# Attention and expert kernel on one core: a planner's cost, a new order of the work, and a shorter count at the end

## The chip, the cores and the metric

The kernel runs on one core of one Trainium2 chip. The metric is the device time of one execution in microseconds (us). The core has five instruction queues that run side by side: TensorE (PE in the profile; its weight loads have a row of their own, PEld), VectorE (DVE), ScalarE (ACT), GpSimd (POOL) and SyncE (SP), which here issues nearly all transfers (DMAs). An engine works through its queue in order; a semaphore holds an instruction until what it needs is there.

## The reference, cut to what matters

```python
# q: 4 x 12288 x 128, kv: 4 x 384 x 32 x 128 (H x W x C)
k = v = kv.reshape(B, H//4, 4, W//4, 4, C).mean(axis=(2, 4)).reshape(B, -1, C) @ w_sr     # 768 keys
a = softmax(q @ k.T / sqrt(C));  x = a @ v                        # 49152 tokens x 128
logits = x @ w_gate                                               # 8 experts
e = argmax(logits);  gate = softmax(logits)[e]
out = gate * (relu(x @ w1[e]) @ w2[e])                            # 1024 hidden units
```

## The kernel before, in words

The tokens are cut into 96 blocks of 512, 24 for each of the four batches `b`; a block is called `t` here. For a block the kernel

- loads q (`qr`, line 987), splits it on POOL into a high and a low f16 part (`qp`, lines 1001 and 1003), and has a transfer on SP turn it (`qT`, line 1005, a DMA transpose: "a turning"; line 1081 is the same for x);
- forms scores on PE in three steps of two matmuls (`s.t.0` to `s.t.2`, L387 into tile `s`), the exponent on ACT (`e`, line 1020), and on DVE `r` (line 1022), which leaves out what a second-moment matrix `M` gives;
- sums the values on PE in four parts (`po`), splits them (`xp`, on ACT and DVE or, by a switch, on POOL) and turns them (`x`);
- runs the batch's usual expert on PE: hidden units `ph.t.0` to `ph.t.2` into one of two PSUM banks (tile `b`), `relu` on ACT and POOL (`gf`, `gh`, `g`), and the way back `py.t`, also in a bank `b`;
- multiplies by the gate on DVE (`ys`, line 1148, tile `y`) and stores on SP (`out_dram<-y`, line 1151).

Beside the blocks runs the work for the next batch: its kv is loaded in three groups of four 512 KB transfers (line 453), pooled, and made into keys (`KT`), and its expert's units are sorted and gathered. For batch 0 this stands at the start: pairs of loaded tiles are added on DVE (`two`, line 463), PE sums and turns them (`pt`, into tile `s`, 16 records each), and the keys follow by way of ACT (`pT`), PE (`pk`, matmul `b<-pT,wsr`), ACT (`vT`) and DVE. Matmuls on `slots` are fillers that keep PE going while it has nothing else.

Tokens whose expert is another one are counted and done by `general_step`, three times within the program (for batches 0 to 2), and in a loop at the end as often as a count `n_left` says. The count: `lp` holds numbers per partition, PE sums them over partitions (`pc`, line 1269), DVE copies them (`left`) and makes numbers of steps (`steps`, `ends`, `n_left`, lines 1489 to 1495); then every engine reads `n_left`, and the program ends.

The order of the instructions of all engines is made before the launch by a planner (`Plan`). Every piece of work is an `op` with an engine, an estimated duration, a due time, what it needs and gives, and its buffers. `Plan.order` (line 170 on) is a list scheduler: on each engine it takes, among the ops that can start, the one with the earliest due time, and gives out buffers in that order. The table `NUDGE` shifts due times by kind of op, by block, or for one op; the table `WAYS` says for some ops which engine does them (`u` of a block: its third group of hidden units is checked and left out of `py`; `x`: the split of x on POOL; `l`: the logits' copy on DVE; `a`, `b`, `c`, `d`: single conversions per batch). For a turning the planner adds to its time on SP half of the time by which the transfers already issued reach beyond the next 2.5 us:

```python
end = free[o.eng] = start + o.us + (0.5 * max(0.0, moved - start - 2.5) if o.eng == "SP" and 1.2 < o.us < 1.8 else 0.0)
```

Here `moved` is the time at which the planner thinks that all transfers issued so far have moved. Nothing of the planner runs on the chip: only its order does.

Of the kernel before, what the change touches and what calls it, by code (L numbers as in the profile page):

```python
# [73 lines left out]
mw:-29.5 nofl:-2.5 o:140 ok.48:-85.5 own2:-13 own?.48:-25 pT.2:14.5 pU:9 pX:0.5 pd:-48 perm.5:12 perm.6:-46 pf.72:-110
pl:-39.5 po.1:1.5 po.2:0.5 pooled.1:3.5 px:-14 qTh:7 qh:3 qp:3 qr:180.5 r.0:-39.5 r.1:0.5 rest:21.5 rs:-7.5 se:-9
see:-68 some0:30.5 sum.0.2.1:2 sum.1.1.1:-6 sum.1.2.0:-2 sum.1.3.0:3.5 sum.2.2.0:-1 sum.2.2.1:4.5 sum.2.3.0:1.5
sure.0:4.5 uy:10.5 uy0:15 w:-29.5 w1l:33.5 w2U:-9.5 w2h:4.5 ws0:-70.5 x:15 xh:1.5 xl:-23.5 ys:0.5 =D.0:-15.5
=D.13:-0.5 =D.5:8 =Lh.3:33.5 =Ms.0:-124.5 =drs.13:-24 =e.10.0:-20 =e.37.1:-2 =e.53.2:9 =e.84.0:20.5 =fl.28:15.5
# [5 lines left out]
=lg.58:-13.5 =lg.8:3 =lgc.3:10 =lp.1.24:53 =mk.1.24:2 =mk2.3.72:16 =mom.3:10.5 =own.3:6.5 =own2.1:7 =pW.2:7 =pX.0:12.5
=pY.3:4 =perm.0.3:-13.5 =perm.0.4:-36.5 =perm.0.5:-14 =perm.0.7:-32.5 =perm.3.5:-2.5 =ph.11.1:8 =ph.15.0:-6
=ph.20.2:-3.5 =ph.21.2:17.5 =ph.24.0:-1 =ph.25.0:-2 =ph.26.1:6.5 =ph.30.0:-29 =ph.35.2:3.5 =ph.37.0:2 =ph.38.2:-3
=ph.39.0:-1.5 =ph.45.1:11 =ph.46.0:12.5 =ph.46.2:-3 =ph.47.2:1 =ph.48.0:10 =ph.49.1:-9.5 =ph.50.1:6.5 =ph.51.0:4.5
=ph.57.0:-7.5 =ph.58.0:-5.5 =ph.59.1:2.5 =ph.6.2:1.5 =ph.61.0:3 =ph.61.1:0.5 =ph.61.2:-2 =ph.64.1:-5.5 =ph.65.0:-6.5
# [1473 lines left out]
```

## Time and profile before

| | us |
|---|---|
| median of 3 runs | 786.45 (785.96 to 789.99) |
| profiled execution | 786.58 |
| its span | 784.5 |
| PE busy in the span | 739.5 (94%) |
| DVE, ACT, POOL busy | 639.1, 588.0, 577.3 |

The span runs from the first instruction to the last; 2.08 us of the profiled execution lie around it. The granted PE clock is at its upper level (2.4 GHz) throughout, except in the last 3.5 us, in which PE has no work. A wait in brackets in a timeline is the idle time of the engine before the instruction, and who ended it.

### The profile page before, as it was taken

What the parts mean: (1) busy time and instruction counts of PE and PEld (TensorE: products, weight loads), DVE (VectorE), ACT (ScalarE), POOL (GpSimd) and SP (SyncE); (2) the same over time, 40 slices, a digit from 0 to 9 for tenths busy, and PEclk for the clock granted to TensorE, in tenths of its full rate; (3) what the DMA queues carried; (4) which work ended last, traced back from release to release, by engine and by line L of the source; (5) the groups of instructions that cost most, each with busy time, mean ns of one, the idle gap of its engine ahead of it and who ended that gap; (6) DMA issues with size and microseconds to landing.
All of it is one profiled execution on the core that took longest, in us unless ns stands there. A gap on an engine that the chain in (4) does not pass through costs nothing.

```text
span 784.5 us, 21744 instructions
## 1 busy us (share of the span) xinstructions
PE 739.5 (94%) x8399; PEld 580.3 (74%) x8399; DVE 639.1 (81%) x1262; ACT 588.0 (75%) x968; POOL 577.3 (74%) x803
## 2 busy tenths in 40 slices
PE   5997999999999899999999899999999999999995
PEld 5675776887777677778776776878877777787774
DVE  5789876889988888868968888688898898767685
ACT  1367778879778777777787787778878787878783
POOL 0357879878789888886779978888656957686662
PEclk9999999999999999999999999999999999999999
DMA  9676989995798999797569899799575889668441
GB/s 341 166 204 115 223 191 204 198 199 114 156 231 175 228 205 264 154 210 134 122 139 225 205 240 248 158 192 192 136 166 106 171 176 200 151 122 166 93 105 56
DMA packets 326168, 138.90 MB, mean 177 GB/s; under 512 B 212478, under 2 KB 318082, under 8 KB 326064
## 3 DMA queue, kind: packets, MB, share of 16 engines
q1 hardware_dynamic: 325584, 137.27, 78.0%
q8 instruction: 66, 1.08, 0.6%
q14 instruction: 38, 0.31, 0.1%
q0 software_dynamic: 192, 0.17, 0.1%
q10 hardware_dynamic: 288, 0.07, 0.0%
HBM read 59.12 MB, written 26.94 MB: 110 GB/s over the span
## 4 chain that ended last, share of the span: by engine, by line
PE 64%; DVE 9%; ACT 8%; DMA 8%; POOL 5%; issue 3%; SPq 0%; ACTq 0%; POOLq 0%; DVEq 0%
PE b L387 31%; PE po L387 19%; PE s L387 13%; DMA qT<-qp 4%; DVE r L1022 4%; ACT e L1020 3%; POOL kv L478 1%; DMA x<-xp 1%; DMA kv<-in_kv_dram 1%; DMA gp<-in_q_dram,gi 1%; ACT X L1113 1%; ACT g L1121 1%; DVE y L1148 1%; DVE xp L1057 1%; ACT junk L742 1%
## 5 line engine op out<-in xcount | busy, mean ns | idle before, releaser
L1022 DVE SCALAR_TENSOR_TENSOR r<-s,e 128x1024 bf16<-128x1024 f32 x288 | 346.8, 1217 | 63.7 <-ACT e L1020 61.6
L1020 ACT ACTIVATE e<-s 128x1024 f32<-128x1024 f32 x288 | 292.1, 1029 | 62.6 <-PE s L387 59.0
L387 PE MATMUL po<-v,r 128*128 128x145 f16 x2304 | 251.4, 227 | 2.6 <-DVE xp L1057 1.7
L387 PEld LDWEIGHTS <-r 128*128 128x128 bf16 x2304 | 167.0, 98 | 26.7 <-issue 4.9
L387 PE MATMUL s<-qT,KT 128*128 128x512 f16 x576 | 166.8, 379 | 11.6 <-DVE r L1022 7.7
L387 PE MATMUL b<-w2U,g 128*128 128x128 f16 x1664 | 156.5, 219 | 1.0 <-POOL g L1117 0.6
L387 PE MATMUL b<-x,w1U 128*128 128x512 f16 x465 | 139.4, 379 | 9.0 <-ACT g L1121 4.7
L387 PE MATMUL po<-M,qT 128*128 128x136 f16 x1152 | 130.9, 223 | 0.0
L387 PE MATMUL b<-L,x 128*128 128x128 f16 x1116 | 123.0, 219 | 1.1 <-ACT g L1121 0.7
L1003 POOL TENSOR_TENSOR qp<-qr,qp 128x512 f16<-128x512 f32 x94 | 108.9, 1159 | 15.6 <-DVE gi L1314 2.0
L1117 POOL TENSOR_TENSOR g<-X,g 128x512 f16<-128x512 f32 x94 | 108.8, 1158 | 10.8 <-DVE gg L1451 4.1
L387 PEld LDWEIGHTS <-g 128*128 128x128 f16 x1664 | 109.0, 98 | 1.9 <-POOL g L1117 1.4
L387 PEld LDWEIGHTS <-qT 128*128 128x128 f16 x1152 | 84.5, 98 | 27.6 <-issue 5.1
L1121 ACT ACTIVATE g<-b,zb 128x512 f16<-128x512 f32 x128 | 87.5, 692 | 18.3 <-PE b L387 15.3
L1001 POOL CAST qp<-qr 128x512 f16<-128x512 f32 x94 | 58.7, 625 | 47.7 <-DMA qr<-in_q_dram 25.3
L387 PEld LDWEIGHTS <-x 128*128 128x128 f16 x1116 | 80.9, 98 | 16.8 <-issue 5.4
L387 PEld LDWEIGHTS <-KT 128*128 128x128 bf16 x576 | 51.3, 99 | 48.0 <-issue 14.1
L1113 ACT ACTIVATE X<-b,zb 128x512 f32<-128x512 f32 x94 | 65.2, 696 | 19.5 <-PE b L387 19.5
L478 POOL TENSOR_TENSOR kv<-kv,kv 128x512 f32<-128x512 f32 x54 | 68.0, 1272 | 15.4 <-DMA kv<-in_kv_dram 6.1
L1115 POOL CAST g<-X 128x512 f16<-128x512 f32 x94 | 58.2, 620 | 28.3 <-ACT X L1113 13.1
L387 PEld LDWEIGHTS <-w1U 128*128 128x128 f16 x480 | 45.2, 98 | 40.5 <-issue 9.2
L1148 DVE TENSOR_TENSOR y<-b,gt 128x512 f32<-128x512 f32 x96 | 65.2, 680 | 7.8 <-PE b L387 5.8
(376 smaller groups left out, 961.2 us busy)
## 6 DMA issues: line engine op xcount, KB each, us to landing
qr<-in_q_dram SPq DMA_DIRECT2D x96, 256.0 KB, 3.4
out_dram<-y SPq DMA_DIRECT2D x96, 256.0 KB, 2.7
kv<-in_kv_dram SPq DMA_DIRECT2D x41, 512.0 KB, 6.1
raw<-in_moe_w_dram SPq DMA_DIRECT2D x14, 512.0 KB, 5.1
e<-in_kv_dram SPq DMA_DIRECT2D x3, 512.0 KB, 9.1
v_dram<-vT SPq DMA_DIRECT2D x4, 384.0 KB, 3.1
qT<-qp SPq DMA_TRANSPOSE x94, 3.6
x<-xp SPq DMA_TRANSPOSE x91, 3.5
```

The lines of the kernel that those rows point to most:

```text
L387: return nc.tensor.matmul(o, l, r, start=start, stop=stop)
L478: nc.gpsimd.tensor_add(flat(to), flat(to), flat(of))
L742: op("ACT", 1.25, lambda j=j, junk=junk: nc.scalar.activation(junk.tile, krow.tile, AF.Sign, bias=key(j), scale=-1.0, accum_out=lc(j)), at ...
L1001: op("POOL", .62, lambda: nc.gpsimd.tensor_copy(qp.tile[:, 0], qr.tile), T - 1.9 * LEN, [("qr", t)], [("qh", t)], [qr, qp])
L1003: op("POOL", 1.17, lambda: nc.gpsimd.tensor_sub(qp.tile[:, 1], qr.tile, qp.tile[:, 0]), T - 1.8 * LEN, [("qh", t)], [("qp", t)], [qr, qp])
L1020: op("ACT", 1.03, lambda e=e, ps=ps: nc.scalar.activation(e.tile, ps.tile, AF.Exp), at + .6, [("s", t, s)], [("e", t, s)], [ps, e])
L1022: op("DVE", 1.22, lambda e=e, ps=ps, s=s: nc.vector.scalar_tensor_tensor(r.tile[:, 2 * s:2 * s + 2], ps.tile, 1.0, e.tile, op0=ALU.add, op ...
L1113: op("ACT", .69, lambda ph=ph, zu=zu: nc.scalar.activation(gf.tile, ph.tile, AF.Relu, bias=zu()), at + .5, [("ph", t, u), ("zb", b)], [("g ...
L1115: op("POOL", .62, lambda: nc.gpsimd.tensor_copy(gg.tile[:, 0], gf.tile), at + 1.5, [("gf", t)], [("gh", t), ("g", t)], [gf, gg])
L1117: op("POOL", 1.16, lambda: nc.gpsimd.tensor_sub(gg.tile[:, UH], gf.tile, gg.tile[:, 0]), at + 2, [("gf", t), ("gh", t)], [("g", t)], [gf, gg])
L1121: op("ACT", .69, lambda u=u, ph=ph, zu=zu: nc.scalar.activation(gg.tile[:, u], ph.tile, AF.Relu, bias=zu()), at + .5, [("ph", t, u), ("zb" ...
L1148: op("DVE", .69, lambda: nc.vector.tensor_tensor(y.tile, py.tile.rearrange("p (c d) -> p c d", d=C), bc(gr["gt"].tile[:, 0, js], C), op=AL ...
```

## The change

The cost of a turning behind transfers that are backed up is counted in full (factor 1 for 0.5), the last op `rest` gets a landing time, and `NUDGE` and `WAYS` hold other numbers, so that all five queues stand in another order. `WAYS` has 63 blocks with `u` for 64, 39 with `x` for 35, 46 with `l` for 50; `a3` and `c3` are gone, `d0` stands for `d3`. The counts, which are whole numbers below 257, are read by PE as the upper halves of their f32 words, in bf16, in `pc` and in two products of `general_step` (`pb`, `pr`); the copy `left` and the number of steps take one instruction less each; the last block (t = 95) is multiplied and stored in two halves, the second of them issued by ACT.

```diff
-L:46.5 M:-43.5 cbc:25 cg:237.5 e.0:3.5 e.1:3 e.2:-1.5 ex:47.5 g:0.5 gate:31 general.0.done:17 general.0.h4:10
+KT:-91 L:37 Ls:6.5 Mh:22.5 con:8.5 drs:-37 e.0:3 e.1:4.5 e.2:-2.5 ex:79.5 fl:2.5 g:0.5 gate:23.5 general.0.pa:-58
...
-            end = free[o.eng] = start + o.us + (0.5 * max(0.0, moved - start - 2.5) if o.eng == "SP" and 1.2 < o.us < 1.8 else 0.0)
+            end = free[o.eng] = start + o.us + (max(0.0, moved - start - 2.5) if o.eng == "SP" and 1.2 < o.us < 1.8 else 0.0)
...
+        parts = [slice(0, CH)] if t < NBLK - 1 else [slice(0, CH // 2), slice(CH // 2, CH)]
+        def scaled():
+            for cs in parts:
+                nc.vector.tensor_tensor(y.tile[:, cs], py.tile.rearrange("p (c d) -> p c d", d=C)[:, cs],
+                                        bc(gr["gt"].tile[:, 0, js], C)[:, cs], op=ALU.mult)
+        def stored():
+            for cs, eng in zip(parts, (nc.sync, nc.scalar)):
+                eng.dma_start(ov[t][:, cs], y.tile[:, cs])
...
         def total():
             for i, (lp, _) in enumerate(lps):
-                mm(pc.tile[:, :E1], ones, lp.tile, i == 0, i == len(lps) - 1)
+                mm(pc.tile[:, :E], ones_b, lp.tile.bitcast(BF16)[:, 1::2][:, :E], i == 0, i == len(lps) - 1)
+            for i, (lp, _) in enumerate(lps):
+                n = lp.tile.bitcast(BF16)[:, 1::2][:, E:E1]
+                mm(pc.tile[:, P:P + E], ones_b, n.to_broadcast([P, E]), i == 0, i == len(lps) - 1)
...
-            nc.vector.tensor_copy(left[:, 2 * b * E:(2 * b + 1) * E], pc.tile[:, :E])
-            nc.vector.tensor_scalar(left[:, (2 * b + 1) * E:2 * (b + 1) * E], ones[:, :E], pc.tile[:, E:E1], None, op0=ALU.mult)
+            nc.vector.tensor_copy(left[:, 2 * b * E:2 * (b + 1) * E].rearrange("p (i e) -> p i e", i=2),
+                                  pc.tile[:, :2 * P].rearrange("p (i e) -> p i e", i=2)[:, :, :E])
...
-        part("PE", .2, lambda: mm(pb.tile[:, :1], below, cnt(), True, True), ["search"], "pb", [gp, pb])
+        part("PE", .2, lambda: mm(pb.tile[:, :1], below_b, half(cnt()), True, True), ["search"], "pb", [gp, pb])
...
-        part("PE", .8, lambda: mm(pr.tile[:, :NT], sel0(), tab(), True, True), ["select"], "pr", [gp, pr])
+        def picked():
+            mm(pr.tile[:, :NJ], half(sel0()), half(tab(0, NJ)), True, True)
+            mm(pr.tile[:, NJ:NT], sel0(), tab(NJ, NT), True, True)
+        part("PE", .45, picked, ["select"], "pr", [gp, pr])
...
-        nc.vector.tensor_scalar_add(steps_i, left, float(TAIL - 1))
-        nc.vector.tensor_single_scalar(steps_i, steps_i, TAIL.bit_length() - 1, op=ALU.arith_shift_right)
-        nc.vector.tensor_copy(steps, steps_i)
+        nc.vector.tensor_scalar(steps, left, (TAIL - 1) / 2, float(TAIL << 23), op0=ALU.add, op1=ALU.add)
+        nc.vector.tensor_scalar(steps, steps, float(TAIL << 23), 1.0 / TAIL, op0=ALU.subtract, op1=ALU.mult)
```

Three places show what the new order does. The first is PE at the start, where the last tiles of batch 0 are summed into tile `s` from `kv`, `raw`, `r` or `e` (buffers that serve as kv's first homes), and `b<-pT,wsr` makes keys of a summed pair. Before:

```order
L387 MATMUL s_242<-ident,r_183 128x128 x8
L387 MATMUL s_205<-ident,e_174 128x128 x8
L387 MATMUL b_282<-pT_278,wsr 128x256
L993 MATMUL b_287<-ident,qr_200 128x128 x4
L387 MATMUL b_297<-pT_284,wsr 128x256
L993 MATMUL b_304<-ident,qr_198 128x128 x4
```

and now:

```order
L391 MATMUL b_239<-pT_223,wsr 128x256
L997 MATMUL b_241<-ident,qr_195 128x128 x4
L391 MATMUL s_229<-ident,e_182 128x128 x8
L997 MATMUL b_263<-ident,qr_199 128x128 x4
L391 MATMUL b_270<-pT_268,wsr 128x256
L391 MATMUL s_204<-ident,r_197 128x128 x8
```

Before, the last two sums stood one behind the other, and two key products behind them; now one sum and one key product (not shown, behind fillers) are left for the end, and the turnings of q for blocks 0 and 1 (`qr`) stand ahead.

The second is SP in the middle, at the first kv loads for batch 3, with turnings of q (`qT`) and x around them. Before, for blocks 51, then 47, 50 and 48:

```order
L1005 DMA_TRANSPOSE qT_7232<-qp_6930 128x8x128
L453 DMA kv_7286<-in_kv_dram 128x1x1024
L453 DMA kv_7294<-in_kv_dram 128x1x1024
L453 DMA kv_7299<-in_kv_dram 128x1x1024
L1081 DMA_TRANSPOSE x_7316<-xp_7230 128x8x128
L1005 DMA_TRANSPOSE qT_7369<-qp_7096 128x8x128
L453 DMA kv_7419<-in_kv_dram 128x1x1024
L1081 DMA_TRANSPOSE x_7421<-xp_7367 128x8x128
```

and now, for blocks 50 and 47, then 51 and 48:

```order
L1009 DMA_TRANSPOSE qT_7235<-qp_6856 128x8x128
L1085 DMA_TRANSPOSE x_7282<-xp_7233 128x8x128
L457 DMA kv_7301<-in_kv_dram 128x1x1024
L457 DMA kv_7316<-in_kv_dram 128x1x1024
L457 DMA kv_7328<-in_kv_dram 128x1x1024
L457 DMA kv_7354<-in_kv_dram 128x1x1024
L1009 DMA_TRANSPOSE qT_7360<-qp_7065 128x8x128
L1085 DMA_TRANSPOSE x_7460<-xp_7362 128x8x128
```

The turning of x that stood between the loads now stands ahead of them, and all four loads stand in a row ahead of the next turning of q.

The third is DVE at the end: the last parts of `relu` (`X`, `g`), the gate (`gt`), the multiplications `y` of the blocks 95 and 94, and the counts. Before:

```order
L1109 TENSOR_TENSOR g_14073<-X_14137,g_14073 128x512
L1179 RECIPROCAL gt_14075<-gt_14075 128x4
L1148 TENSOR_TENSOR y_14178<-b_14103,gt_14075 128x512
L1148 TENSOR_TENSOR y_14184<-b_14142,gt_13884 128x512
L1274 COPY left<-b_14180 128x8
L1275 TENSOR_SCALAR left<-ones,b_14180 128x8
L1489 TENSOR_SCALAR steps_i<-left 128x64
L1490 TENSOR_SCALAR steps_i<-steps_i 128x64
L1491 CAST steps<-steps_i 128x64
L1492 SCALAR_TENSOR_TENSOR ends<-steps 128x64
L1495 TENSOR_TENSOR n_left<-ends,step 128x1
```

and now:

```order
L1156 TENSOR_TENSOR y_14183<-b_14106,gt_14064 128x256 x2
L1253 SCALAR_TENSOR_TENSOR mo_13480<-lg_10969,mo_13480 128x16
L1255 SCALAR_TENSOR_TENSOR code<-mo_13480 128x16
L1269 TENSOR_TENSOR junk_14190<-code,lists 128x144
L1271 TENSOR_REDUCE lp_14191<-junk_14190 128x9
L1156 TENSOR_TENSOR y_14199<-b_14148,gt_13996 128x512
L1291 COPY left<-b_14194 128x16
L1514 TENSOR_SCALAR steps<-left 128x64
L1515 TENSOR_SCALAR steps<-steps 128x64
L1516 SCALAR_TENSOR_TENSOR ends<-steps 128x64
L1519 TENSOR_TENSOR n_left<-ends,step 128x1
```

The gate of block 95 is computed before `g` now, the last count (`lp`) stands between the two multiplications, and two instructions fewer stand behind the last of them.

## Rows read from the trace of the kernel before

**Rows 1.** The page's first part: busy time, share of the span, instructions.
```profile
PE 739.5 (94%) x8399; PEld 580.3 (74%) x8399; DVE 639.1 (81%) x1262; ACT 588.0 (75%) x968; POOL 577.3 (74%) x803
```

**Rows 2.** Busy time by stretch: length, engines' busy us (instructions), clock, DMA share, GB/s.
```profile
100.00:500.00 400.00, 380.93 (x4402) 298.56 (x4400) 331.26 (x629) 313.69 (x515) 333.31 (x439) 1.00 0.87 192
500.00:740.00 240.00, 237.88 (x2789) 188.68 (x2787) 201.63 (x373) 195.73 (x321) 170.40 (x241) 1.00 0.76 158
```

**Rows 3.** PE's groups of matmuls: busy, mean ns, idle before them, who ended it.
```profile
L387 PE MATMUL s<-qT,KT 128*128 128x512 f16 x576 | 166.8, 379 | 11.6 <-DVE r L1022 7.7 <-DMA qT<-qp 3.2
L387 PE MATMUL b<-x,w1U 128*128 128x512 f16 x465 | 139.4, 379 | 9.0 <-ACT g L1121 4.7 <-ACT X L1113 1.9 <-DVE X L1106 0.9
```

**Rows 4.** Tile qT: its turnings on SP (min/median/max ns), and their landing.
```profile
L1005 SPq DMA_TRANSPOSE qT<-qp x94: 1231/1262/5228, 26.3 to 743.8; - x94
...
DMA to landing us min/median/max: 3.0/3.6/8.5
```

**Rows 5.** SP's timeline at batch 3's first kv loads: start, us, instruction.
```profile
409.74 1.89 SPq L453 DMA_DIRECT2D kv<-in_kv_dram  x3
411.73 1.37 SPq L1081 DMA_TRANSPOSE x<-xp  x1
413.88 4.09 SPq L1005 DMA_TRANSPOSE qT<-qp  x1
```

**Rows 6.** PE's timeline in the same place.
```profile
421.56 0.60 PE L387 MATMUL s<-qT,KT 128*128 128x512 f16 x2 [1.01 <-DMA qT<-qp]
```

**Rows 7.** Transfers between 409 and 421 us.
```profile
DMA packets 4192, 2.70 MB, mean 225 GB/s; under 512 B 3760, under 2 KB 3760, under 8 KB 4190
```

**Rows 8.** PE's groups again: the products of the counts, and two bf16 or f16 neighbours.
```profile
L387 PE MATMUL b<-slots 128*128 128x384 f16 x84 | 16.2, 325 | 0.7 <-DVE con L523 0.5
...
L387 PE MATMUL b<-gp 128*128 128x388 f32 x6 | 2.6, 508 | 0.0
...
L387 PE MATMUL b<-lp,ones 128*128 128x9 f32 x10 | 1.6, 246 | 0.2
...
L387 PE MATMUL b<-gp,below 128*128 128x1 f32 x6 | 0.9, 217 | 0.0
...
L387 PE MATMUL b<-u,ones_q 128*128 128x1 bf16 x4 | 0.7, 167 | 0.0
```

**Rows 9.** DVE's timeline at the start: the last sum of a pair.
```profile
20.59 1.22 DVE L463 TENSOR_TENSOR e<-e,e 128x1024 f32<-128x1024 f32 x1
```

**Rows 10.** PE's timeline at the start: the last two sums.
```profile
21.17 1.95 PE L387 MATMUL s<-ident,r 128*128 128x128 f32 x16
22.95 1.95 PE L387 MATMUL s<-ident,e 128*128 128x128 f32 x16
```

**Rows 11.** Transfers in the first 20 us.
```profile
DMA packets 2896, 6.80 MB, mean 340 GB/s; under 512 B 369, under 2 KB 1360, under 8 KB 2896
```

**Rows 12.** Busy time in two stretches at the end, columns as in rows 2.
```profile
766.00:778.30 12.30, 9.36 (x119) 6.89 (x116) 7.89 (x24) 5.39 (x9) 3.27 (x15) 1.00 0.14 44
778.30:784.50 6.20, 0.61 (x4) 0.52 (x4) 2.01 (x9) 0.00 (x0) 0.00 (x0) 0.72 0.29 86
```

**Rows 13.** DVE's timeline at the end.
```profile
777.64 1.33 DVE L1148 TENSOR_TENSOR y<-b,gt 128x512 f32<-128x512 f32 x2 [0.70 <-POOL gt L1183]
...
779.12 0.23 DVE L1275 TENSOR_SCALAR left<-ones,b 128x8 f32<-128x8 f32 x1
...
779.84 0.20 DVE L1491 CAST steps<-steps_i 128x64 f32<-128x64 int32 x1
...
780.39 0.16 DVE L1495 TENSOR_TENSOR n_left<-ends,step 128x1 int32<-128x1 f32 x1
```

**Rows 14.** PE's timeline at the end: the last matmuls of block 94's way back.
```profile
777.79 0.44 PE L387 MATMUL b<-w2U,g 128*128 128x128 f16 x5
```

**Rows 15.** Tile y from 776 us on: its two stores on SP, and their landing.
```profile
L1151 SPq DMA_DIRECT2D out_dram<-y x2: 372/488/604, 778.4 to 779.0; - x2
...
DMA to landing us min/median/max: 2.5/2.5/2.6
```

More of the change, by code (lines that the diff above doesn't have):

```diff
@@ L74 @@
[L74 to L78, printed above, removed]
@@ L84 @@
[L84 to L88, printed above, removed]
@@ new lines @@
+kv.0.2:20 kv.1.0:14.5 kv.1.2:29 kv.1.3:41.5 kv.2.1:-9 kv.2.2:11.5 kv.2.3:37.5 less.1:226 lgc:-3.5 lp.48:98.5
+mean:164.5 mk0.48:-8.5 mk1.92:75.5 mw:-4 o:83 ok.48:-65 own:78 pL:6 pT.2:-2 pT2:-12.5 pW:-49 pY:-9.5 pd:6 perm.2:-43
+perm.5:17.5 pf.24:-5.5 pf.72:-94 pg:0.5 pk.0:-2.5 pl:-5 po.0:0.5 po.1:1.5 po.2:0.5 pown:-2.5 qTh:-34 qh:3.5 qp:3
+qr:210.5 r.0:-296.5 r.2:-4 rest:16.5 se:-5 see:-78 some0:51 sum.0.2.0:3 sum.0.2.1:10 sum.0.3.0:5 sum.1.1.0:-10.5
+sum.1.1.1:-11.5 sum.1.2.0:-6.5 sum.1.2.1:-5.5 sum.1.3.0:3 sum.2.1.1:-40.5 sum.2.3.0:3 sure.0:11.5 sure.24:14.5
@@ new lines @@
+=general.1.ph4:-16.5 =general.2.ph0:-5.5 =general.2.ph4:15 =general.2.pr:6 =general.2.pv:11.5 =general.2.py:-24
+=gf.70:24 =gf.85:22.5 =gh.23:-95 =gh.37:5.5 =gh.45:-9.5 =gh.67:12.5 =known.3.72:-8.5 =kv.0.1.2:-9 =kv.0.1.3:-13.5
+=kv.0.2.1:13 =kv.0.2.2:19 =kv.0.2.3:-35.5 =kv.1.0.0:-8 =kv.3.1.3:-25 =less.0.0:14 =lg.3:12.5 =lg.33:1.5 =lg.55:12
+=lg.60:-10.5 =lg.81:2.5 =lg.88:1 =lg.89:-5.5 =lgc.8:12.5 =lp.1.24:65.5 =mk.1.24:14 =mk1.1.24:13.5 =mw.1:-0.5
+=own?.0.0:-16 =own?.2.48:-31 =pL.1:-25.5 =pL.3:-7 =pT2.0:32 =pX.0:6.5 =pd.2:3 =perm.0.5:-13 =pf.1.24:1 =ph.11.1:6.5
@@ new lines @@
+=s.93.2:1 =s.94.2:10.5 =se.17:8 =sum.1.0.2.1:2 =sum.1.0.3.0:8.5 =sum.1.1.2.1:-18.5 =sum.1.2.2.1:-7 =sum.2.0.2.1:-0.5
+=sum.2.1.2.0:-1 =sum.2.2.3.1:2.5 =sum.3.0.2.1:-6 =sum.3.1.2.1:17.5 =sure.1.24:-18.5 =uy.0:12 =w2l.2:28 =w2m.0:4.5
+=within.3.1:27.5 =wm.0:102.5 =ws.0:2 =ws0.2:-121 =x.32:20.5 =xh.86:-6.5 =xh.93:-11.5 =xh.95:-6 =xl.5:28 @0:-113.5
+@1:-204 @10:2 @11:-0.5 @12:-1.5 @13:2 @14:-4 @15:-1 @16:-1.5 @17:5.5 @18:-1.5 @19:-4.5 @20:-3.5 @21:1.5 @22:-1 @23:0.5
+@26:-1 @27:-1.5 @28:-1 @29:0.5 @3:7 @30:-1 @31:3.5 @32:-7.5 @33:-3.5 @34:-1 @35:-6 @36:-1.5 @37:-2.5 @38:5 @39:6.5
@@ L112 @@
+@4:-4 @40:1.5 @41:-2 @42:-1.5 @44:-1.5 @45:-4.5 @46:-2.5 @47:-2 @48:-3 @49:-2 @50:1.5 @51:-3 @52:-0.5 @54:-1.5 @55:0.5
+@57:16.5 @58:1.5 @59:-1.5 @6:-2 @61:-1.5 @62:-3.5 @63:1 @64:-3 @65:-1.5 @66:-6 @67:-2 @68:-1 @7:-2 @71:-2.5 @72:7
+@73:-1 @74:-11.5 @78:7 @79:-3 @80:-2 @81:-2.5 @83:1 @84:-2 @89:-4 @9:-1 @90:-1 @91:-4 @92:4 @93:-11
 """.split())}
 WAYS = dict.fromkeys("""
[L114 to L115 removed]
@@ L340, in attention_moe @@
     nc.vector.memset(code, 0.0)
-    left, steps, steps_i = keep("left", [P, NL]), keep("steps", [P, NL]), keep("steps_i", [P, NL], I32)
+    left, steps = keep("left", [P, NL]), keep("steps", [P, NL])
     nc.vector.memset(left, 0.0)
@@ L1351, in general_step @@
         cnt = lambda: tab(NJ - 1, NJ)
+        half = lambda x: x.bitcast(BF16)[:, 1::2]
         def search():
@@ L1519, in attention_moe @@
                 marks(b, START + (t + 3) * LEN, t + 1 - LAST, t + 1, True)
-            op("DVE", 1.1, count_steps, START + (t + 5) * LEN + 3, [("left", b)], [("steps", b)], lock=True)
+            op("DVE", .85, count_steps, START + (t + 5) * LEN + 3, [("left", b)], [("steps", b)], lock=True)
             if b in STEPS_AFTER:
@@ L1523, in attention_moe @@
     op("DVE", .3, rest_steps, START + (NBLK + 5) * LEN,
-       [("steps", B - 1)] + [("stored", b) for b in range(B)] + [("general", b, "find2") for b in STEPS_AFTER], ["rest"])
+       [("steps", B - 1)] + [("stored", b) for b in range(B)] + [("general", b, "find2") for b in STEPS_AFTER], ["rest"], lands=1.4)
     def fill(b):
```

76 lines of the change are left out of this document (35 added, 41 removed).

## Prediction

> **What bounds the kernel now.** I read the page's first part, then the busy time by stretch, then the groups of PE's matmuls with what ended the idle time before them, then the timelines of the places found.
>
> PE is busy for 739.5 of the span's 784.5 us [rows 1], so 45 us is all that an order can win while PE's work stays the same. By stretch the idle time is uneven: from 100 to 500 us, where kv loads for the next batches run, PE idles 400 - 380.93 = 19.1 us, or 4.8 per 100 us; from 500 to 740, with none of these loads, 240 - 237.88 = 2.1 us, or 0.9 per 100 [rows 2]. At the later rate the first stretch would have 3.5 us idle, so some 15 us hang on the loads. The rest lies at the start and the end. The groups of matmuls say what PE waited for: the scores 11.6 us, of which DVE ended 7.7 and turnings of q 3.2; the hidden units 9.0 us, mostly ACT, which empties the two banks [rows 3].
>
> The turnings are what the planner's cost is about. One takes 1.26 us of SP in the median and 5.2 at most, and lands after 3.6 us in the median and 8.5 at most [rows 4]. At batch 3's first kv loads one can watch it: three loads and a turning of x are issued, and the turning of q behind them holds SP for 4.09 us [rows 5]; the scores that need it begin at 421.56, after PE has waited 1.01 us [rows 6]. SP is in order, so what stands behind such a turning waits too.
>
> **The change part by part.** The sum is made against the profiled execution, 786.58 us (span 784.5 and 2.08 around it), which is 0.13 above the median of the runs.
>
> *Planner's factor and `rest`.* They run nowhere on the chip and cost nothing; only the order counts, below.
>
> *Counts in bf16.* In each of the three steps within the program, the product of 388 columns takes 2.6 / 3 = 0.87 us of PE and the one-column product 0.9 / 3 = 0.30 (both f32, two records each) [rows 8]. The nearest narrow rows: 384 f16 columns take 16.2 / 84 = 0.19, one bf16 column 0.7 / 4 = 0.17 [rows 8]. New: 0.19, plus the four columns left in f32 at the price of the one-column f32 product, 0.30, plus 0.17 for the other: 0.66 for 1.17, so 0.5 less, three times: -1.5. `pc` is 1.6 / 5 = 0.32 per partial count [rows 8] and becomes two bf16 products, at most 2 x 0.17: nothing. One block more runs its third group of units through `py`: four matmuls at 0.44 / 5 = 0.09 [rows 14], up to 0.35, of which 0.2 is taken, as in a full stream they overlap. Together -1.3. All of this is PE time, on the path wherever PE is not waiting; bounds -1.7 (all three steps in full, nothing back) and 0 (each step stands in a wait).
>
> *Other switches.* Four x splits more on POOL, four fewer on DVE, and a few copies between ACT and DVE. POOL is busy 74% and DVE 81% [rows 1], and what covers these edits is PE's own work, 95% of the stretch of the loads [rows 2]. I take nothing; what they cost if a split comes late is in the slower rival.
>
> *The start.* Before, after the last pair's sum on DVE (to 21.81) [rows 9] PE still had two sums of 1.95 us in a row, to 24.90 [rows 10], and two key products. Now one of each is left for the end, which is 1.95 us less on the chain to the first scores. In return a q load (256 KB) stands ahead of the last kv load on SP: at the 340 GB/s of these 20 us [rows 11], 0.77 us. Net -1.2. Bounds: -3.2, if DVE's sum of 1.22 drops out of the chain as well; +0.8, if PE's sums were covered and only the q load counts. Fillers take what PE has free, so nothing else moves.
>
> *The last two blocks.* From 766 to 778.3 us PE is busy for 9.36 of 12.30 us [rows 12]: 2.9 us idle, while hidden units wait for banks and DVE puts marks and counts between. The new order computes gate 95 earlier and puts marks behind copies that PE needs; the hidden units still go through two banks. I take a quarter, -0.7; bounds -2.9 (all of it) and +0.7 (one multiplication `y` of 1.33 / 2 more on the path [rows 13]).
>
> *The count at the end.* Block 94's last matmul ends at 778.23 [rows 14], its `y` at 777.64 + 1.33 = 778.97 [rows 13]. With an earlier gate, `y` of 95 (its two halves, and four small instructions of the last count) falls under block 94's matmuls, but `y` of 94 still needs them: 778.23 + 0.67 is the same 778.9. The halves cost one fixed start more, hidden there; if that cover is gone, some 0.2. Behind `y` the second `left` (0.23, overlapping the first) and the cast (0.20) go [rows 13]: about 0.35 less until `n_left`, which ended at 780.55. The last store is issued at 779.0 and lands 2.6 us later, at 781.6 [rows 15], a microsecond after `n_left`; behind both come the waits of the program's end, to 784.5. So what is late next is that store. I take -0.3; bounds -0.4 and 0 (the store sets the end).
>
> On that store a page of the Trainium skill speaks against the halves. The row: two stores from one queue, 0.6 us apart, both land in 2.5 to 2.6 us [rows 15]. The Trainium skill (DMA: Bandwidth & Descriptors, "Issuing engines are not separate DMA queues") says that DMAs of all engines run on the same 16 DMA engines, and that issuing from several saves only issue time. If ACT's queue were a path of its own, the end would come up to 0.4 us (half a store's issue) earlier; by that rule it comes no earlier, as block 94's store, still whole and issued last, is behind the same engines. No run here has shown two queues at once.
>
> *The order in the middle.* What I can price are the direct waits of PE for turnings, 3.2 us in all [rows 3]. Where the order now has a turning ahead of loads such a wait goes; at batch 3's first loads it does not simply go, it passes from block 50 to block 51, now behind four loads in a row. I take half: -1.6. Bounds: -6 (also some of the waits that turnings pass on through DVE and ACT, towards the 15 us) and +9 (the slower rival).
>
> Sum: -1.3 - 1.2 - 0.7 - 0.3 - 1.6 = -5.1, so 781.5 by the profiled execution, 781.4 by the median.
>
> **The rivals.**
>
> *The middle stays as it is* (783.1 = 786.6 - 3.5). For it: PE's waits for ACT, 4.7 + 1.9 us, and DVE, 7.7 [rows 3], are waits for banks and score buffers of which there are two each, and no number of buffers changes. Against it: the waits pile up where the loads are [rows 2]. The Trainium skill (Perfetto Trace Analysis, "Optimization Strategy") says that a gap repeating on an engine that should be saturated can mean too few PSUM buffers; by that rule an order wins none of these waits, and the time is this rival's. The trace agrees for the hidden units, where ACT ends most waits, and not for the dependence on loads.
>
> *The change does not do what it says* (785.0 = 786.6 - 1.3 - 0.3): the same bytes move through the same 16 engines, busy 87% of the stretch [rows 2], so turnings only swap who waits; the earlier q load eats the gain at the start, the end gains nothing but the count. One or two bad places of the next rival lead to 787.7 at most. For it: SP's order at batch 3. Against it: the start's chain is shorter by a count of instructions.
>
> *Slower, by loads in a row.* The nine groups of four 512 KB loads stand ahead of turnings that PE needs soon. At the 225 GB/s of such a place [rows 7] a load more in a row is 2.3 us more for the turning behind it. To lose 0.5% (3.9 us) after the other gains of 3.5 takes 7.4 / 2.3, so four of the nine places; then 786.6 - 3.5 + 4 x 2.3 = 792.3. For it: at batch 3 the fourth load has moved ahead of the turning, and block 51's scores come two pieces of work after block 50's on PE. Against it: elsewhere SP's order mostly has three loads before a turning, as before.
>
> **How the numbers follow.** About 0.5%, 3.9 us, is what a measurement of this kernel can tell from no change: faster is below 782.5, slower above 790.4. My forecast has 0.48 (its own range 776.5 to 782.5), the unchanged middle 0.24 (0.04 of it below 782.5), the change that does little 0.16, slower 0.12. That gives faster 0.52, same 0.36, slower 0.12. The range, 775.5 to 788.0, leaves out the slower rival and some 0.04 below.
>
> **What would show it.** The start: PE's last sum from `ident` ends near 23.7 instead of 24.90, and the first scores begin about 1.2 us earlier. Counts: the 388-column group is gone, and 384 bf16 columns take about 0.19. The end: the idle time in PE's last 12 us falls below 2.9, and `n_left` ends about 1.2 us after the last `y` ends, not 780.55 - 778.97 = 1.6. The middle: PE's idle time from 100 to 500 falls below 19, and turnings' waits before scores below 3.2. The forecast is wrong if that stretch keeps its 19 us or gains some, or if the first scores do not come earlier.

## The result, and the profile after

The changed kernel takes 797.07 us (median of 5 runs, 796.38 to 799.08), the kernel before 787.61 in the same five rounds: a ratio of 1.0117 (95% interval 1.0094 to 1.0140). It is slower by 9.5 us, outside the range given. The profiled execution took 799.08 us, the longest of the five; its span is 797.3, so 12.8 more than before. PE is busy for longer, though it has less to compute [rows 1]. The page's first part:

```profile
PE 745.7 (94%) x8403; PEld 583.2 (73%) x8403; DVE 635.0 (80%) x1247; ACT 592.6 (74%) x973; POOL 579.1 (73%) x809
```

The two stretches of [rows 2], at the same amount of PE's work (103 to 513 us and 513 to 754.5): idle are 410 - 385.16 = 24.8 us for 19.1, and 241.5 - 237.55 = 3.9 for 2.1.

```profile
103.00:513.00 410.00, 385.16 (x4453) 301.14 (x4451) 333.01 (x623) 315.06 (x523) 327.07 (x436) 1.00 0.88 188
513.00:754.50 241.50, 237.55 (x2776) 188.97 (x2775) 199.50 (x367) 197.32 (x318) 172.62 (x247) 1.00 0.77 157
```

PE's groups of matmuls, against [rows 3, 8]: the scores wait as before (11.2 us, 3.1 of them for turnings), the hidden units too, but now also behind the copy `Ms`; the wait of the way back for POOL's `g` has grown to 3.9 us from 0.6. The product of 388 f32 columns has become one of 384 in bf16 and one of 4 in f32. The way back before:

```profile
L387 PE MATMUL b<-w2U,g 128*128 128x128 f16 x1664 | 156.5, 219 | 1.0 <-POOL g L1117 0.6 <-DVE g L1109 0.3
```

and the groups after:

```profile
L391 PE MATMUL s<-qT,KT 128*128 128x512 f16 x576 | 166.7, 380 | 11.2 <-DVE r L1026 7.0 <-DMA qT<-qp 3.1 <-ACT kv L740 0.2
L391 PE MATMUL b<-w2U,g 128*128 128x128 f16 x1668 | 157.2, 219 | 3.9 <-POOL g L1121 3.9
L391 PE MATMUL b<-x,w1U 128*128 128x512 f16 x465 | 138.7, 379 | 10.3 <-ACT Ms L884 2.5 <-ACT g L1125 2.4 <-DVE X L1110 1.3
...
L391 PE MATMUL b<-gp 128*128 128x384 bf16 x3 | 1.0, 333 | 0.0
...
L391 PE MATMUL b<-gp 128*128 128x4 f32 x6 | 0.8, 210 | 0.0
...
L391 PE MATMUL b<-gp,below_b 128*128 128x1 bf16 x3 | 0.5, 167 | 0.0
```

Tile `qT` [rows 4]: the turnings of q hold SP as long as before and land no earlier. Over all 196 turnings of q, x, keys and values, the time on SP beyond 1.26 us each sums to 62.8 us, for 65.7 before.

```profile
L1009 SPq DMA_TRANSPOSE qT<-qp x94: 1231/1248/5324, 28.0 to 757.5; - x94
...
DMA to landing us min/median/max: 3.0/3.8/9.5
```

To find where the time went I compared at equal work: for each matmul of a trace, the time to the start of the next, less the interval usual for its shape in a full stream (55.5 ns for 128 columns of 16 bits, 63 for 145, 215.5 for 512, 110 for 128 of f32). The rest is PE's loss: idle time, and matmuls at half the clock. The columns are stretches of work done, in us of those intervals; `*` marks a profile in which PE's clock fell to half in that stretch, once per mark (3.4 us long, but 6.8 in the first stretch of `done_later` and `repaired2`). The lower level at the very start, which every profile has, bears no mark. All kernels but `before` and `code_alone` have the new order or a repair of it.

```
                0-60    60-140  140-160  160-280  280-340  340-400  400-440  440-680   680-   sum
before          22.2      7.5      1.6     12.2      6.6      6.3      4.8     12.1     5.1   78.3
code_alone      21.7      7.5      1.3     12.6      6.6      6.2      3.4     12.6     5.3*  77.3
after           24.9**    7.0      6.3*    10.7     11.4      6.2      7.3     14.1     4.1   92.0
loads_paired    20.5      8.0      4.8     10.8     10.9      5.4      7.5     14.2     4.1   86.2
done_later      22.9*     7.0      4.8     10.5      9.3      5.4      8.0     14.2     4.1   86.2
repaired2       23.5*     6.0      6.2     10.4      9.5      5.3     10.7*    14.0     4.1   89.6
```

The work itself is 697.8 us before and 696.6 after. So 13.7 us of loss less 1.2 of work give 12.5 of the 12.8; the times differ by 9.5 us, as this execution is the longest of its five. Each row is one profile. `loads_paired` and `done_later` have the same instructions in the same order at 60 to 140 and differ by 1.0 there without a fall of the clock, so a difference below about 1 us between two rows says nothing. The loss stands in the start (+2.7), in 20 us of work around batch 1's weights (+4.7), at 280 to 340 (+4.8), at 400 to 440 (+2.5) and later (+2.0); elsewhere the new order gains a little (-3.1).

Three times PE's granted clock fell to its lower level of 1.2 GHz; in the profile of before it did not fall while PE worked, once it had risen. A table of two-us stretches (length, PE's busy us, clock, DMA share, GB/s) shows one, behind 2.88 us of idle time; the others are at 78 to 84 and 191 to 196 us:

```profile
12.00:14.00 2.00, 0.00 (x0) 1.00 1.03 410
14.00:16.00 2.00, 1.73 (x8) 0.56 1.03 410
16.00:18.00 2.00, 2.00 (x13) 0.58 1.07 375
18.00:20.00 2.00, 2.00 (x19) 1.00 1.05 357
```

Each is worth 2 x 0.44 + 2 x 0.42 = 1.7 us of full clock, together 5.1 us of this execution.

At the very start the clock column can't be read this way. It prints 1.00 ahead of the profile's first record of the clock, but the first sums run at the lower level there: 16 f32 matmuls of 128 columns take 3.75 us, and 1.95 later. Before, this lasted until 13.1 us. So the clock was not at its upper level throughout, as I wrote ahead of the prediction, but only from there on.

### The profile page after: what moved, and what is told of

It is laid out like the page before. It is cut to its first block, busy times and chain, and to the rows that moved or that the text cites. A ratio compares the mean times of both kernels' runs of the same rounds, so it can differ in the third digit from the quotient of the medians.

```text
span 797.3 us, 21749 instructions
## 1 busy us (share of the span) xinstructions
PE 745.7 (94%) x8403; PEld 583.2 (73%) x8403; DVE 635.0 (80%) x1247; ACT 592.6 (74%) x973; POOL 579.1 (73%) x809
## 3 DMA queue, kind: packets, MB, share of 16 engines
q8 instruction: 66, 1.08, 0.6%
## 4 chain that ended last, share of the span: by engine, by line
PE 55%; DVE 13%; POOL 9%; ACT 9%; DMA 7%; issue 5%; SPq 1%; POOLq 0%; ACTq 0%; DVEq 0%
PE b L391 26%; PE po L391 16%; PE s L391 11%; DVE r L1026 6%; ACT e L1024 4%; DMA qT<-qp 3%; POOL kv L482 2%; DMA kv<-in_kv_dram 2%; POOL g L1121 2%; ACT g L1125 1%; DMA raw<-in_kv_dram 1%; DVE y L1156 1%; DVE xp L1061 1%; POOL g L1119 1%; POOL xp L1066 1%
## 5 line engine op out<-in xcount | busy, mean ns | idle before, releaser
L391 PE MATMUL s<-qT,KT 128*128 128x512 f16 x576 | 166.7, 380 | 11.2 <-DVE r L1026 7.0
L391 PEld LDWEIGHTS <-w1U 128*128 128x128 f16 x480 | 45.6, 99 | 43.2 <-issue 10.7
L1156 DVE TENSOR_TENSOR y<-b,gt 128x512 f32<-128x512 f32 (+1 forms) x97 | 65.5, 678 | 11.9 <-PE b L391 10.4
```

The source lines that it names most:

```text
L391: return nc.tensor.matmul(o, l, r, start=start, stop=stop)
L1156: nc.vector.tensor_tensor(y.tile[:, cs], py.tile.rearrange("p (c d) -> p c d", d=C)[:, cs], bc(gr["gt"].tile[:, 0, js], C)[:, cs], op=ALU. ...
```

## Experiments

Moves of single instructions are written as pairs: the operation that gives the first name is taken out of the planned order and put back just ahead of the one that gives the second. Nothing else changes.

```diff
-        for o in self.order():
+        for o in moved(self.order()):
+def moved(seq):
+    for what, ahead in MOVES:
+        o = seq.pop(at(what))
+        seq.insert(at(ahead), o)
+    return seq
```

**Code or order.** `code_alone` has the new code with the old tables and costs; `order_alone` the old code with the new ones. The changed lines are those of the diff.

> The kernel before with the four changes of the code (counts in bf16, one copy for the lists, three instructions for the steps, the last block's y in two halves on two queues), but with the old tables, the old factor and the old costs, so that the order on every engine is that of before. Theory 'order': the code saves the 1.4 us of PE worked out from rows 8 and a little at the end, so about 786, 1.2 to 2 below the kernel before. Rival 'code': the split store or the new products hold something up, and the 10 us lost are here: 790 or more.

> The old code in the order of the changed kernel (its tables, its factor, its costs). Theory 'order': all of the loss and none of the gain of the code, 797.1 + 1.4 = 798.5. Rival 'code': about the time before, 790 at most.

`code_alone`: 787.37 us for 787.95 before, ratio 0.9994 (0.9969 to 1.0018); its profile has 1.5 us less work and 1.0 less loss. `order_alone`: 798.56, ratio 1.0119 (1.0092 to 1.0146). The loss is the order's. The code's gain, by its work about 1.5 us, is too little to show in the times.

**Costs or tables.** `rule_alone` has the old tables and code with the new costs, `tables_alone` the new tables and code with the old costs.

```diff
-            end = free[o.eng] = start + o.us + (0.5 * max(0.0, moved - start - 2.5) if o.eng == "SP" and 1.2 < o.us < 1.8 else 0.0)
+            end = free[o.eng] = start + o.us + (max(0.0, moved - start - 2.5) if o.eng == "SP" and 1.2 < o.us < 1.8 else 0.0)
```

> The kernel before with only the planner's two costs changed (the factor 1.0 in place of 0.5 for turnings behind transfers, and 1.4 us of landing for the last step), the tables and the code old: the order is planned anew on every engine. Theory 'new deal': the tables were fitted to the old costs, so the new order is not better anywhere in particular and costs 3 to 12 us: 791 to 800. Rival 'truer rule': by better counted turnings PE's waits for them (3.2 us) and for what hangs on them go down, 784 to 787.

> The changed kernel with its new tables and new code, planned by the old costs (factor 0.5, no landing for the last step). If tables and costs are one thing, as the 849.5 of rule_alone suggests, the order falls apart here as well: 30 to 60 us above 797. Rival 'the old rule was the better one': by the old costs the new tables give an order at least as good, 790 to 798.

`rule_alone`: 849.52 us, ratio 1.0778 (1.0754 to 1.0802), far above what either theory gave. `tables_alone`: 830.07 (two runs), ratio 1.0541 (1.0501 to 1.0581), in the range of its theory. So the four corners are 788 (old, old), 850 (old tables, new costs), 830 (new tables, old costs), 797 (new, new): tables and costs are one thing, and a cost changed by itself deals every engine's order anew. PE in `rule_alone`, its page and its scores:

```profile
PE 759.1 (90%) x8408; PEld 586.2 (69%) x8408; DVE 642.7 (76%) x1262; ACT 592.7 (70%) x968; POOL 579.2 (68%) x803
...
L387 PE MATMUL s<-qT,KT 128*128 128x512 f16 x576 | 166.3, 379 | 25.8 <-DVE r L1022 17.5 <-DMA qT<-qp 7.4
```

The same of `tables_alone`:

```profile
PE 752.9 (91%) x8403; PEld 584.0 (70%) x8403; DVE 632.9 (76%) x1247; ACT 592.0 (71%) x973; POOL 581.7 (70%) x809
...
L391 PE MATMUL s<-qT,KT 128*128 128x512 f16 x576 | 165.6, 379 | 19.2 <-DVE r L1026 13.7 <-DMA qT<-qp 4.3 <-ACT kv L740 0.2
```

The turnings' time beyond 1.26 us falls to 54.6 us in `rule_alone`, while PE's waits grow everywhere, for turnings too (7.4 for 3.2): less time of SP in turnings is not what PE waits for.

**The first loads.** In the changed kernel the two loads for DVE's second sum are the fifth and the seventh. DVE's sums and what PE made of them:

```profile
6.67 1.23 DVE L467 TENSOR_TENSOR kv<-kv,kv 128x1024 f32<-128x1024 f32 x1 [2.64 <-DMA kv<-in_kv_dram]
12.99 1.23 DVE L467 TENSOR_TENSOR raw<-raw,raw 128x1024 f32<-128x1024 f32 x1 [2.61 <-DMA raw<-in_kv_dram]
```

```profile
14.27 3.65 PE L391 MATMUL s<-ident,raw 128*128 128x128 f32 x16 [2.88 <-DVE raw L467]
...
25.91 1.95 PE L391 MATMUL s<-ident,r 128*128 128x128 f32 x16
```

`loads_paired` puts the two loads of each sum together:

```diff
+MOVES = [("kv.0.2.0", "kv.0.0.3"), ("kv.0.2.1", "kv.0.0.3"), ("kv.0.0.2", "kv.0.1.1"),
+         ("kv.0.1.0", "kv.0.2.3"), ("kv.0.1.2", "kv.0.2.3")]
```

> The changed kernel with only SP's first ten kv loads in another order: the two loads that one DVE sum needs stand together, in the order in which PE takes the sums. Theory 'pairs': the second pair is complete after four loads, not seven, at 1.28 us a load (512 KB at 410 GB/s), so its sum on DVE begins near 9.5 us, not at 12.99; PE's idle time of 2.88 us at 11.4 goes, and with it the half clock of 14.4 to 17.8; the time falls by 2.5 to 4.5, to 792.5 to 794.5. Rival 'last load': the first scores wait for the last pair anyway, and the time stays within 1 us of 797.1.

Measured: 793.06 us, ratio 1.0068 (1.0042 to 1.0094), so 4.0 us less than the changed kernel. The second sum begins at 9.73 on DVE, and PE does not wait for it:

```profile
9.73 1.23 DVE L479 TENSOR_TENSOR raw<-raw,raw 128x1024 f32<-128x1024 f32 x1 [0.95 <-DMA raw<-in_kv_dram]
```

```profile
11.56 2.34 PE L403 MATMUL s<-ident,raw 128*128 128x128 f32 x16
...
23.07 1.95 PE L403 MATMUL s<-ident,r 128*128 128x128 f32 x16
```

The last sum ends at 25.0 for 27.9, and the first scores begin at 29.66, for 32.49 in the changed kernel and 31.39 before. The stretch 0 to 60 loses 20.5 us, 1.7 less than before. Theory 'pairs' holds for the wait and for the clock. Four profiles have this wait, 2.5 to 3.3 us long: the changed kernel's, `order_alone`, `ls_first` and `tables_alone`. In all four the sums behind it run at half the clock. In the changed kernel the clock had risen at 10.8 us and fell again; in the other three it rises only at 20.2 to 20.9 us. In the nine profiles without the wait it rises at 12.2 to 14.4 us and stays up for the sums that follow. `order_alone`, where the sum behind the wait and most of the next still take nearly twice 1.95 us:

```profile
14.81 3.78 PE L391 MATMUL s<-ident,raw 128*128 128x128 f32 x16 [2.47 <-DVE raw L467]
18.38 3.17 PE L391 MATMUL s<-ident,kv 128*128 128x128 f32 x16
```

Its first scores begin at 34.33 us.

**Batch 1's weights.** The wait of 2.02 us before hidden units, which the profile puts down to `Ms` on ACT:

```profile
185.24 1.15 ACT L849 ACTIVATE w1h<-row,ws 128x1024 f16<-128x1024 f32 x1 [0.34 <-POOL row L847]
186.29 0.99 ACT L740 COPY kv<-s 128x1024 f32<-128x1024 f32 x1
187.32 1.15 ACT L746 ACTIVATE junk<-kv,sg 128x1024 bf16<-128x1024 f32 x1
...
188.47 1.92 ACT L1024 ACTIVATE e<-s 128x1024 f32<-128x1024 f32 x2
190.27 0.37 ACT L884 ACTIVATE Ms<-b,ws 128x128 f32<-128x128 f32 x1
```

```profile
190.69 0.38 PE L391 MATMUL b<-x,w1U 128*128 128x512 f16 x1 [2.02 <-ACT Ms L884]
```

`ls_first` takes that bank's wait away:

```diff
+MOVES = [("Ls.1", "less.1.0"), ("Ls.2", "less.2.0"), ("Ls.3", "less.3.0")]
```

> The changed kernel with one instruction of ACT moved in batches 1 to 3: the copy Ms<-b (line 884 in the changed kernel), which frees one of the two banks of the hidden units, now stands ahead of the first sign count of its batch, not behind it and two exponentials. Theory 'bank': the wait of 2.02 us before the hidden units at 188.7 falls below 0.5, that at 381.4 (0.44) goes, and the half clock of PE at 191.9 to 195.1, which follows the first wait, does not come; 797.1 falls by 2 to 4, to 793 to 795. Rival 'ACT is full': the work between is only put off, the wait shows up at the next bank or score, and the time stays within 1 us of 797.1.

Measured: 798.10 us, ratio 1.0125 (1.0100 to 1.0150), no gain. The bank comes free 3 us earlier, and PE waits 2.46 us at the next scores instead, for `r`. Ahead of that `r` DVE is idle too, and waits for the exponential on ACT:

```profile
189.58 2.36 DVE L1038 SCALAR_TENSOR_TENSOR r<-s,e 128x1024 bf16<-128x1024 f32 x2 [0.64 <-ACT e L1036]
```

```profile
190.86 0.81 PE L403 MATMUL s<-qT,KT 128*128 128x512 f16 x2 [2.46 <-DVE r L1038]
```

My theory 'bank' fell; the rival 'ACT is full' held: the exponentials that the scores need start at 188.54 on ACT, for 188.47 in the changed kernel. The half clock behind the wait came all the same. That DVE is full with weights at the same time was my next theory. `spread` pulls the work of both apart, on top of `loads_paired`:

```diff
+MOVES += [("krow.1", "pL.1"), ("s.19.2", "pL.1"), ("e.19.2", "pL.1"), ("r.19.2", "w1l.1"), ("w1h.1", "w1l.1"),
+          ("Ls.1", "w1l.1"), ("less.1.0", "e.21.0"), ("zp.1", "lm.1"), ("w2l.1", "lm.1")]
```

> The kernel of the run loads_paired with batch 1's weights work pulled apart at 181 to 191 us: on PE one pair of scores ahead of the product of row with itself, on ACT the copy kv<-s first, then an exponential, then w1h, Ms, and the first sign count three exponentials later; on DVE r ahead of w1l, and zp and w2l behind the next r. Theory 'both full': PE ran dry for 2.0 us (and 2.5 in ls_first) because ACT had 3.3 us and DVE 3.2 us of weights work in a row at the same time; spread out, the idle time in that stretch falls below 1, and 793.1 falls by 1.5 to 2.5. Rival 'put off': the same work must be done somewhere in the next 15 us with DVE and ACT at 80 to 90%, PE waits there, and the time stays within 0.7 of 793.1.

Measured: 797.20 us, ratio 1.0101 (1.0075 to 1.0126): no gain on `loads_paired`, with intervals that overlap. The moves contain a mistake of mine: `w2l` now stands ahead of the small reduction `lm`, for whose product PE waits in its order, 2.53 us. `repaired2`, below, mends it; there PE's waits in the place are 0.25, 0.57, 0.96 and 0.95 us, and the stretch 140 to 160 still loses 6.2 us, for 4.8 without the moves. Pulling the pile apart did not pay here, so that the pile is the cause is not shown.

**The scatter.** POOL's scatter of general step 0 writes to the output, as the stores of `y` do. In the changed kernel it stands right behind block 33's store, issued at 344.66 and landed at 347.34, and POOL is idle for 4.34 us in front of it:

```profile
348.27 1.09 POOL L1508 DMA_INDIRECT out_dram<-pool,gi  x1 [4.34 <-DVE r L1026]
```

(DVE had long been done. The scatter waits for a semaphore that this store sets; in seven profiles, the one before among them, it stands right behind the store and begins 0.92 to 0.93 us after the landing.) PE then waits for what stands behind it on POOL:

```profile
353.78 0.33 PE L391 MATMUL b<-L,x 128*128 128x128 f16 x3 [0.62 <-ACT X L1117]
355.13 0.34 PE L391 MATMUL b<-w2U,g 128*128 128x128 f16 x3 [0.97 <-POOL g L1121]
```

`done_later`, on top of `loads_paired`:

```diff
+MOVES += [("general.0.done", "lgc.9")]
```

> The kernel of the run loads_paired with one instruction of POOL moved: the scatter of general step 0 (line 1508 in the changed kernel), which now stands right behind the store of block 33, is put 8 us later, behind the splits and products of blocks 34, 35 and 38. Theory 'scatter': POOL stood idle for 4.34 us because the scatter writes to the output as that store does and waits for its landing (347.34, scatter at 348.27); moved, it finds the store landed, POOL does not wait, the hidden units' second halves g come 4 us earlier, and of PE's idle time between 348 and 358 (3.3 us) at least 2 go: 793.1 falls to about 791. Rival 'covered': DVE and ACT are late there in any case, PE's idle time in that place keeps over 2.5 us, and the time stays within 0.7 of 793.1.

Measured: 793.82 us, ratio 1.0071 (1.0048 to 1.0095): no change in the times. In the place itself POOL's wait falls to 2.56 us, with the store landed 3.5 us earlier, so 1.8 of the 4.34 went; in 1.5 of what is left POOL waits for DVE. Of the two waits of PE one of 0.62 is left:

```profile
349.86 0.34 PE L403 MATMUL b<-w2U,g 128*128 128x128 f16 x3 [0.62 <-POOL g L1133]
```

The stretch 280 to 340 loses 9.3 us for 10.9, and 10.0 and 9.5 in the two later kernels with this move; 0.5 is lost again at 400 to 440. In this profile the clock fell at 74 to 82 us, and the first stretch loses 2.4 us more. Why the median of the times shows no gain either is open.

**All repairs.** `repaired` has the moves of `loads_paired`, `done_later` and `spread`.

> The three repairs together (loads in pairs, scatter later, weights spread). If the theories of the two single runs hold and add up, 793.1 - 2 - 2 = 789; if both rivals hold, 793. What then remains above the kernel before is what the new order costs in other places.

Measured: 794.73 us, ratio 1.0086 (1.0057 to 1.0115): with the mistake in `spread` the sum is worth nothing beyond the loads. `repaired2` mends it and moves three loads:

```diff
-          ("zp.1", "lm.1"), ("w2l.1", "lm.1")]
+          ("zp.1", "xf.19"), ("w2l.1", "xf.19"),
+          ("kv.3.2.1", "kv.3.2.3"), ("kv.3.2.0", "kv.3.2.3"), ("kv.3.2.2", "kv.3.2.3"), ("sum.3.2.1.1", "sum.3.2.1.0")]
```

> The run repaired with its own mistake mended and one repair more. There, the work w2l on DVE had been put ahead of the small reduction u<-Ms, for whose product PE waits in order (2.52 us at 190.5); now zp and w2l stand behind it. In addition three kv loads of batch 3 at 476 us, which stand 7 us behind general step 1's load of 1 MB, go 8 us later. Theory 'three places': PE's idle time near 181 to 193 falls from 2.6 to under 1, near 343 to 354 it keeps the 1.5 gained in done_later, near 468 to 492 it falls from 4.4 to about 3; in sum 4 us below loads_paired where the clock stays up: 789. Rival 'put off': the idle time in these places comes back within 20 us, and the time stays at 792 to 794.

Measured: 797.25 us, ratio 1.0134 (1.0106 to 1.0161), above what the theory gave and above the rival's 792 to 794. At 468 to 492 the waits are 3.7 us for 4.7 in `loads_paired`; but now four loads stand in a row on SP, and the turning behind them (and behind six smaller transfers) makes PE wait 3.55 us, with a fall of the clock after it:

```profile
481.59 3.34 SPq L469 DMA_DIRECT2D kv<-in_kv_dram  x4
```

```profile
498.54 1.03 PE L403 MATMUL s<-qT,KT 128*128 128x512 f16 x2 [3.55 <-DMA qT<-qp]
```

That stretch loses 10.7 us for 7.5: 3.2 us for a place with three loads more in a row, 1.7 of them the fall of the clock. It looks like the prediction's slower rival, but a row of four is not slow by itself: the kernel before has one too, issued at 478.06 us, the turning behind it holds SP for 5.23 us, and no scores wait for it.

**A better order by hand.** `tuned` moves nine instructions of `code_alone` where its trace shows PE waiting behind work that could stand later (`#4`: the fifth of the operations with that name).

```diff
+MOVES = [("less.0.0", "lg.4"), ("r.3.0", "some.0"), ("less.0.1", "po.2.2"), ("r.53.2", "lp.1.24#4"), ("r.13.0", "lg.11"),
+         ("po.9.3", "s.11.0"), ("r.44.2", "some0.2"), ("ys.92", "own?.3.92"), ("po.57.0", "general.1.pq")]
```

> The run code_alone (old order, new code) with nine instructions moved where its trace shows PE waiting behind work that could stand later: two sign counts of batch 0 behind the exponentials that scores wait for (2.6 us idle at 62 to 65), r of block 53 ahead of four list instructions (1.72 at 444), r of block 13 ahead of a copy (1.34 at 130.5), and five more of 0.2 to 0.7. Theory 'waits of PE are worth their length': half of the 7 us named goes, 787.4 falls to 784. Rival 'put off': the slot that scores wait for comes free at the pace of ACT and DVE, each wait returns at the next scores, and the time stays within 1.5 of code_alone.

Measured: 786.98 us for 787.62 before, ratio 0.9989 (0.9969 to 1.0010), no more than `code_alone`. The longest of these waits, in `code_alone`:

```profile
445.75 0.59 PE L387 MATMUL s<-qT,KT 128*128 128x512 f16 x2 [1.72 <-DVE r L1022]
```

In `tuned` it has become three, together 1.37 us:

```profile
446.53 0.59 PE L399 MATMUL s<-qT,KT 128*128 128x512 f16 x2 [0.30 <-DVE r L1034]
447.83 0.22 PE L399 MATMUL b<-lp,ones_b 128*128 128x8 bf16 x2 [0.71 <-DVE junk L1270]
448.41 0.33 PE L399 MATMUL b<-L,x 128*128 128x128 f16 x3 [0.36 <-ACT g L1133]
```

No version measurably better than the kernel before was found.

## Why the prediction was wrong

By its own terms, in the profiled executions:

```
term                   forecast   measured
counts in bf16           -1.3       -1.2   work of PE, 697.8 to 696.6
start                    -1.2       +2.7   loss of the first 60 us of work
last two blocks          -0.7       -1.0   loss of the last 17 us of work
count at the end         -0.3        0.0   from the last y to the end, 5.58 to 5.61 us
order in the middle      -1.6      +12.0   the rest of the loss (13.7 - 2.7 + 1.0)
```

*Counts:* right in size. By the rows after, the products of 384, of 4 and of 1 column take 0.33, 0.27 and 0.17 us a step, 0.77 for 1.17, so 0.4 less and not 0.5: the 384 bf16 columns cost 0.33, not the 0.19 of the fillers. The bound of -1.7 should have been -1.5 by its own rows (3 x 0.5).

*The start* failed in its net, "-1.2", and beyond its bound of +0.8. I looked at the end of the chain (one sum of 1.95 us less behind the last pair) and at one load in front of the last pair, and did not ask which loads stand in front of the second. That pair had moved from the fifth load to the seventh, and the price was in the rows: at the 340 GB/s of [rows 11] a load of 512 KB takes 1.5 us, so two loads are 3.1, and the second sum came 2.1 us later (12.99 for 10.90). Nor was there a term for the clock, which I took to be up from the first matmul on. Of the loss in the first stretch 2 x 1.7 us were its falls, one behind this wait and one at 78 us. With the loads in pairs the stretch loses 1.7 us less than before, and the kernel is 4.0 us faster than the changed one.

*The last two blocks:* the forecast number came, idle in PE's last 12 us is 10.30 - 8.06 = 2.2 us (the two us ahead of this row are all busy) for 2.9 [rows 12]. But `code_alone`, with the old order, loses 5.3 there, of which 1.7 are a fall of the clock, so 3.6 without it: that the new order gains here is not shown.

```profile
780.60:790.90 10.30, 8.06 (x99) 5.84 (x97) 6.96 (x24) 4.72 (x8) 4.00 (x16) 1.00 0.21 60
```

*The count at the end:* between the last `y` and `n_left` lie 1.06 us, for 1.58 [rows 13], and the end comes no earlier. That the store sets it, the bound I gave as 0, fits, but no run took the store away.

```profile
791.01 0.69 DVE L1156 TENSOR_TENSOR y<-b,gt 128x512 f32<-128x512 f32 x1
...
792.60 0.16 DVE L1519 TENSOR_TENSOR n_left<-ends,step 128x1 int32<-128x1 f32 x1
```

The halves, one on SP and one on ACT, 0.3 us apart, took 3.4 us to land here, the whole store behind them 2.4 ([rows 15]: 2.5):

```profile
L1161 SPq DMA_DIRECT2D out_dram<-y x2: 372/372/372, 789.7 to 791.7; - x2
L1161 ACTq DMA_DIRECT2D out_dram<-y x1: 407/407/407, 790.0 to 790.0; - x1
...
DMA to landing us min/median/max: 2.4/3.4/3.4
```

That is no price of two queues: in `code_alone`, with the same halves on SP and ACT 0.3 us apart, all three stores land in 2.3 us.

```profile
L1157 ACTq DMA_DIRECT2D out_dram<-y x1: 407/407/407, 776.2 to 776.2; - x1
...
DMA to landing us min/median/max: 2.3/2.3/2.3
```

In both kernels block 94's whole store, issued last, lands last. The Trainium skill (DMA: Bandwidth & Descriptors, "Issuing engines are not separate DMA queues") says that DMAs from different engines run on the same 16 DMA engines; no run here decides whether ACT's queue is a path of its own.

*The order in the middle* failed in sign, and its upper bound of +9 was too low. I priced it by the waits for turnings that the change speaks of, took half of 3.2 us as won, and let every other place of PE stay as it was. Measured in the profile, the waits for turnings did not change (3.1 us), and 12.0 us of other loss came, 1.7 of them the one fall of the clock there (10.6 in `loads_paired`, without any). Of this, 0.9 to 1.6 us is the scatter behind a store, by three profiles (10.0, 9.3 and 9.5 at 280 to 340, for 10.9), though no time shows it. Some 3 us more around batch 1's weights are in every profile of the new order. The 2.7 us more at 400 to 440 are in those of the new order with the new code, but only some 0.7 in `order_alone`. Moving the work of these places repaired neither; what causes them, and the 2 us behind 440, stays open. An order from a new search is a new order everywhere, as `rule_alone` shows at its worst, and the step "half of 3.2" had no row for that.

*The rivals:* loads in a row, 0.12, had the right sign, but it is not what made this change slow, and its price of 2.3 us a load was too high by the one place that shows it (1.1 in `repaired2`, three loads more for 3.2 us with the clock's fall). 'The middle stays' was wrong in the sum, though the scores' waits, 11.2 us for 11.6, did stay. The Trainium skill (Perfetto Trace Analysis, "Optimization Strategy") says that a gap repeating on the engine that should be saturated can mean too few buffers. That these waits outlived a new order, and that one came back in three pieces in `tuned`, is in keeping with it; no run here had more buffers, so it is not shown.

## What to carry to other kernels

Where a change brings a new order from a search, ask of each in-order queue what its first consumers need first, and give the forecast a term for all the places that no edit names: here those cost 12 us in the profile, where the waits that the change was about held 3.2. Read the clock from the length of known matmuls where the profile has no record of it yet. A table fitted to a planner's costs does not carry over to other costs: here either mix of old and new was 33 to 62 us slower than the pair that belongs together. A local wait removed in a kernel whose PE waits on two buffers each is not a gain until the sum over the next 20 us says so.
